# Retention and a top-1 mixture of experts on one core: logits with tokens on partitions, an ordered TensorE stream, joined routing, VectorE work spread over both products

## The chip, the cores and the metric

One core of a Trainium2 chip runs the whole program. The metric is the device time of one execution in microseconds (us). Engines are named as in the profile: PE is TensorE (PEld its loads of the stationary operand), DVE is VectorE, ACT is ScalarE, POOL is GpSimd, SP is SyncE, whose queue issues most DMAs.

## What is computed

The reference is a retention layer in blocks of 64, written here without its tables, followed by a mixture of eight experts of which each token takes one:

```python
# batch 4, heads 8, seq 768, head_dim 64; all float32
for b in range(nb):
    qb, kb, vb = (q[:, :, sl], k[:, :, sl], v[:, :, sl])
    intra = (qb @ kb.T * Dmask) @ vb
    inter = (qb * lam_pow) @ kv_state
    out[:, :, sl] = intra + inter
    kv_state = lam_block * kv_state + (kb * rev_pow).T @ vb
x = out.transpose(0, 2, 1, 3).reshape(3072, 512)
logits = x @ w_gate                       # 512 x 8
e_idx = argmax(logits); gate_w = softmax(logits)[e_idx]
eom = 1 / (1 + exp(-(x @ w_output_gate)))
for e in range(8):                        # w1: 512 x 1024, w2: 1024 x 512
    mask = e_idx == e
    out[mask] = gate_w * eom[mask, e] * (relu(x[mask] @ w1[e]) @ w2[e])
```

By the reference's own draw of the inputs the eight experts have 385, 361, 364, 401, 418, 380, 356 and 407 tokens.

## The kernel before

**Retention.** The sequence is cut into 6 chunks of 128 tokens; with 4 batches that makes 24 positions n = 4c + b. A loop over s from -2 to 21 (L1022 on) works on three positions at once, and its tail (L1091 on) does the last ones. An iteration transposes k and q of position s+2 on PE into `pk` and `pq` (`stage_a`, L308), and ACT copies them to `kT` (L315) and `qT` (L317). `stage_d` (L425) makes the gate's logits of position s-1: four products in four column groups of 32, summed later; ACT copies them (`part`, L434). `stage_a2` leaves `qd` (L328) and `kd` (L282) to POOL. `stage_b` (L346) makes the scores of s+1 in two banks, which DVE multiplies by the decay (`at`, L355, two instructions). `stage_e` turns the logits with one PE transpose (L456) and sums the four groups on DVE (L457). `stage_d2` turns x on DVE (L443) and stores it with four SP issues (L448). `stage_c` then adds state times `qd` (L379, not in the first chunk) and v times `at` (L384) in the bank `po`, ACT copies that to `xT` (L392), and PE makes the next state (`pst`, L401), which DVE joins with the old one (L412, L414).

Each engine takes its instructions in program order, so this order is the schedule; Python lists `later` and `ranking`, emptied by `weave`, drop the small routing instructions between the larger ones.

**Routing.** After every fourth position `route_choose` (L467) finds each token's expert on DVE as a one-hot `oh`, casts it and adds it up position by position in `cum` (L497, four adds); `route_place` (L519) gets each token's place in its expert's list from two PE products (`pr`: L535 with the triangle, L536 with ones and `cum`) and scatters a record to a table in HBM. After position 15 `pick_first` (L623, `pfirst`) takes the expert with most tokens so far; its weights are loaded first, and its first 256 columns gathered and turned ahead of the rest (`first_gather` L753, `first_turn`, `first_hi`, `first_lo`). The other seven are sorted by their counts at the end (`sort_rest`).

**Experts.** Every expert p has a fixed number of columns, `CAPS[p]` (L18). The sizes are for the order of picking. Products are made of two parts of each operand, a high one rounded by ACT (L129 for weights, L814 for x, L842 for h) and the rest from DVE (L138, L815, L843), in three products (`mm3`, L78 to L80). Up products fill `ph` in eight steps fc; down products of the experts 1 to 4 are in a turned form, four steps of 24 products of the expert's columns into `py` (read by DVE in L904 and L910), the others give rows of 128 tokens (`pyr`, 512 columns). The next expert's x is turned by `x_turn` (L796) and cut by `x_split` (L814, L815) in the steps of the down product. A token beyond an expert's columns goes to a block after everything (L1232 on) that runs only if a count is over its size.

**Handover** (L1091 to L1164). The first expert's products are a list of units; `fill` puts some of them between the last positions and routing steps.

Of the kernel before, what the change touches and what calls it, by code (L numbers as in the profile page):

```python
# [17 lines left out]
CAPS = (512, 434, 418, 402, 396, 384, 374, 368)  # L18
# [5 lines left out]
def kernel(  # L24
# [17 lines left out]
    P = 128  # L42
# [102 lines left out]

    qkv = {}
    packs = {}
    EARLY = 16


    BLOCKS = (0, 2, 3, 6, 9, 12, 15)

    def load_qkv(n, i0=0, i1=3):
# [4 lines left out]
        if n < EARLY and n not in packs:  # L158
            packs[n] = wpool.tile([P, 4, 512], F32, tag=("whi", "wlo")[n % 2], bufs=4, name=f"qkv_{n}")
        for i, (nm, src) in list(enumerate((("k", k), ("q", q), ("v", v))))[i0:i1]:  # L160
            t = packs[n][:, i, :] if n < EARLY else slot(f"{nm}_{n}")
            rows = src[b, :, c * P : (c + 1) * P, :]
            if nm == "q" and n in BLOCKS:
# [9 lines left out]
    with tc.manual_schedule():  # L173
# [19 lines left out]
        wgs = const.tile([P, NKC, 32], F32, name="wgs")  # L193
        nc.gpsimd.memset(wgs, 0.0)
# [16 lines left out]
    cum = const.tile([P, B + 1, E], BF16, name="cum")  # L211
# [28 lines left out]
    def routing_tables():  # L240
# [16 lines left out]
        nc.gpsimd.memset(cum[:, 0, :], 0.0)  # L257
# [27 lines left out]
    def query_parts(n, pq):  # L285
        if n not in BLOCKS:
            yield slice(0, P), lambda t: t, pq.rearrange("p (g t) -> p g t", g=NPAIR)
            return
# [8 lines left out]
    def stage_a(n):  # L297
# [4 lines left out]
        for src, dst in ((k_in, pk), (q_in, pq)):  # L302
            if n < 2 and (n > 0 or dst is pq):
                keep_warm(1)
            if dst is pq and n in BLOCKS:
                src = src.rearrange("p (h d) -> p h d", h=H)
# [9 lines left out]
        for r, view, src in query_parts(n, pq):  # L316
            nc.scalar.copy(out=view(qT[r]), in_=src)  # L317
        live[n] = dict(kT=kT, qT=qT, qd=None, kd=None)

    def stage_a2(n):  # L320
# [4 lines left out]
        if c > 0:  # L325
            qd = packs[n][:, 3, :] if n < EARLY else slot(f"qd_{n}")
# [43 lines left out]
    def stage_c(n):  # L370
        L = live[n]
        c, b = divmod(n, B)
        vt = qkv[n][2]
        sd = old_state.pop(n, None)
        po = bank(f"po_{n}")

        if c > 0:
            for g in range(NPAIR):
                nc.tensor.matmul(  # L379
                    po[:, g * P : (g + 1) * P], state[b][:, g, :], L["qd"][:, g, :], start=(g == 0), stop=False  # L380
                )
        for g in range(NPAIR):
# [9 lines left out]
        nc.scalar.copy(  # L392
            out=xT.rearrange("p (b g r) -> p g b r", b=4, g=NPAIR),
            in_=po.rearrange("p (g b r) -> p g b r", g=NPAIR, b=4),
        )
# [22 lines left out]
    parts = {}  # L418

    def stage_d(n):  # L420
        xT = live[n]["xT"]
        xTv = xT.rearrange("p (b g r) -> p g b r", b=4, g=NPAIR)
        plg = bank(f"plg_{n}")
        for g in range(NPAIR):
            nc.tensor.matmul(  # L425
                plg[32 * g : 32 * (g + 1), 0:P],
                wgs[:, g, :],
                xTv[:, g],
                start=True,
                stop=True,  # L430
                tile_position=(0, 32 * g),
            )
# [445 lines left out]
    def out_index(p):  # L878
# [6 lines left out]
        if rest:  # L885
            nc.gpsimd.memset(oi, 4 * NOROW)
# [436 lines left out]
```

## Time and profile before

| | before |
|---|---|
| median of 3 runs | 454.27 us (454.0, 454.27, 456.28) |
| the profiled execution | 455.79 us |
| its span | 453.9 us |
| PE busy | 422.8 us, 93% |
| DVE, ACT, POOL busy | 301.5, 191.6 and 263.0 us |
| retention and routing, start of the last position's state product | 143 us |
| first expert's first up product on the second half of its columns | 172.1 us |
| start of the last DMA-only stretch (end of PE) | 448.0 us |

Times in rows of the profile are us from the span's start. A group row reads: line, engine, operation, output <- input, sizes, count | busy us, mean ns of one | idle time of its engine just before and what ended it. A row of the chain reads start, length, engine, tile and line; the count behind it is of passes, and a float32 product has two.

### The profile page before, as it was taken

What the parts mean: (1) busy time and instruction counts of PE and PEld (TensorE: products, weight loads), DVE (VectorE), ACT (ScalarE), POOL (GpSimd) and SP (SyncE); (2) the same over time, 40 slices, a digit from 0 to 9 for tenths busy, and PEclk for the clock granted to TensorE, in tenths of its full rate; (3) what the DMA queues carried; (4) which work ended last, traced back from release to release, by engine and by line L of the source; (5) the groups of instructions that cost most, each with busy time, mean ns of one, the idle gap of its engine ahead of it and who ended that gap; (6) DMA issues with size and microseconds to landing.
All of it is one profiled execution on the core that took longest, in us unless ns stands there. A gap on an engine that the chain in (4) does not pass through costs nothing.

```text
span 453.9 us, 9333 instructions
## 1 busy us (share of the span) xinstructions
PE 422.8 (93%) x3282; PEld 383.2 (84%) x3282; DVE 301.5 (66%) x826; ACT 191.6 (42%) x461; POOL 263.0 (58%) x297
## 2 busy tenths in 40 slices
PE   8798999999939999999999989998998999999994
PEld 5687878887838879899999978997997988988984
DVE  4567586878587954765975686579559676684611
ACT  4554665665705512524344153434424453461400
POOL 6263656674564657774577477757757777412002
PEclk9998999999969999999999998999999999999999
DMA  7998787896993344574464344435534556533001
GB/s 172 223 235 217 192 207 196 199 216 168 200 259 128 92 116 175 152 256 144 124 231 146 116 137 143 140 124 179 196 123 141 173 198 226 175 124 123 16 26 47
DMA packets 109834, 73.21 MB, mean 161 GB/s; under 512 B 76708, under 2 KB 90792, under 8 KB 109777
## 3 DMA queue, kind: packets, MB, share of 16 engines
q1 hardware_dynamic: 101648, 56.07, 44.6%
q0 software_dynamic: 7984, 16.44, 11.3%
q8 instruction: 28, 0.46, 0.4%
q14 instruction: 30, 0.24, 0.2%
q10 hardware_dynamic: 144, 0.00, 0.0%
HBM read 59.47 MB, written 13.62 MB: 161 GB/s over the span
## 4 chain that ended last, share of the span: by engine, by line
PE 61%; DVE 19%; DMA 6%; issue 5%; ACT 4%; POOL 4%; SPq 0%; DVEq 0%; POOLq 0%; ACTq 0%
PE ph_None L79 8%; PE ph_None L80 8%; PE ph_None L78 8%; PE pyr L79 4%; PE pyr L80 4%; PE pyr L78 4%; PE po L384 4%; DVE wlo L138 3%; DVE cum L497 3%; PE po L379 3%; PE ps L346 3%; POOL out_dram L921 2%; DMA out_dram<-yo,outrow 2%; PE pk L308 2%; PE pst L401 2%
## 5 line engine op out<-in xcount | busy, mean ns | idle before, releaser
L732 POOL DMA_INDIRECT xg<-x_d,rows x90 | 94.8, 1053 | 45.5 <-issue 22.6
L79 PE MATMUL ph_None<-xlo,whi 128*128 128x434 f32 (+6 forms) x224 | 77.9, 348 | 5.4 <-DVE xlo L815 5.4
L138 DVE TENSOR_TENSOR wlo<-raw,whi 128x512 fp32r<-128x512 f32 x121 | 80.8, 688 | 1.4 <-ACT whi L129 0.8
L78 PE MATMUL ph_None<-xhi,whi 128*128 128x434 f32 (+6 forms) x224 | 77.8, 347 | 1.2 <-ACT xhi L814 1.2
L80 PE MATMUL ph_None<-xhi,wlo 128*128 128x434 f32 (+6 forms) x224 | 77.3, 345 | 0.0
L129 ACT CAST whi<-raw 128x512 fp32r<-128x512 f32 x128 | 75.1, 614 | 0.0
L921 POOL DMA_INDIRECT out_dram<-yo,outrow x54 | 57.9, 1073 | 16.4 <-issue 14.0
L842 ACT ACTIVATE hhi<-ph_None 128x434 fp32r<-128x434 f32 (+6 forms) x56 | 28.1, 502 | 91.0 <-PE ph_None L80 91.0
L843 DVE SCALAR_TENSOR_TENSOR hlo<-ph_None,hhi 128x434 fp32r<-128x434 f32 (+6 forms) x56 | 32.0, 571 | 51.6 <-ACT hhi L842 51.6
L79 PEld LDWEIGHTS ph_None<-xlo,whi 128*128 128x128 f32 x224 | 42.8, 191 | 7.2 <-DVE xlo L815 6.6
L78 PEld LDWEIGHTS ph_None<-xhi,whi 128*128 128x128 f32 x224 | 42.7, 191 | 3.3 <-ACT xhi L814 2.5
L79 PE MATMUL py<-hlo,whi 128*128 128x434 f32 (+3 forms) x128 | 45.0, 351 | 0.0
L80 PE MATMUL py<-hhi,wlo 128*128 128x434 f32 (+3 forms) x128 | 44.9, 351 | 0.0
L78 PE MATMUL py<-hhi,whi 128*128 128x434 f32 (+3 forms) x128 | 44.9, 351 | 0.0
L80 PEld LDWEIGHTS ph_None<-xhi,wlo 128*128 128x128 f32 x224 | 42.7, 191 | 0.3
L814 ACT CAST xhi<-y 128x256 fp32r<-128x256 f32 (+3 forms) x56 | 17.4, 360 | 58.2 <-DVE y L802 54.8
L985 POOL DMA_INDIRECT out_dram<-yn,table x12 | 13.2, 1098 | 48.5 <-DVE yn L982 37.7
L79 PE MATMUL pyr<-wlo,hhi 128*128 128x512 f32 (+1 forms) x96 | 37.6, 392 | 0.0
L78 PE MATMUL pyr<-whi,hhi 128*128 128x512 f32 (+1 forms) x96 | 37.6, 391 | 0.0
L80 PE MATMUL pyr<-whi,hlo 128*128 128x512 f32 (+1 forms) x96 | 37.5, 390 | 0.0
L584 POOL DMA_INDIRECT tab_d<-rec,idx x24 | 24.5, 1019 | 21.0 <-issue 19.2
L355 DVE TENSOR_TENSOR at<-ps,decay 128x512 f32<-128x512 f32 x48 | 31.7, 684 | 6.3 <-PE ps L346 6.1
(173 smaller groups left out, 849.9 us busy)
## 6 DMA issues: line engine op xcount, KB each, us to landing
raw<-in_moe_w_dram SPq DMA_DIRECT2D x27, 1024.0 KB, 5.2
x_d<-xn SPq DMA_DIRECT2D x80, 64.0 KB, 2.6
qkv<-in_k_dram SPq DMA_DIRECT2D x16, 256.0 KB, 3.1
qkv<-in_v_dram SPq DMA_DIRECT2D x16, 256.0 KB, 4.4
raw<-in_moe_w_dram POOLq DMA_DIRECT2D x3, 1024.0 KB
qkv<-in_q_dram SPq DMA_DIRECT2D x9, 256.0 KB, 4.0
k<-in_k_dram SPq DMA_DIRECT2D x8, 256.0 KB, 3.5
q<-in_q_dram SPq DMA_DIRECT2D x8, 256.0 KB, 3.8
```

The source lines that it names most:

```text
L78: nc.tensor.matmul(ps, a[0], b[0], start=first, stop=False)
L79: nc.tensor.matmul(ps, a[0], b[1], start=False, stop=False)
L80: nc.tensor.matmul(ps, a[1], b[0], start=False, stop=last)
L129: nc.scalar.copy(out=hi, in_=src)
L138: eng.tensor_tensor(out=lo, in0=src, in1=hi.bitcast(F32), op=ALU.subtract)
L355: nc.vector.tensor_tensor(out=at, in0=ps.rearrange("p (g t) -> p g t", g=NPAIR), in1=dec[:, j], op=ALU.mult)
L384: nc.tensor.matmul(po[j * D : (j + 1) * D, g * P : (g + 1) * P], vt[:, 2 * g + j, :], L["at"][j][:, g, :], start=(c == 0), stop=(c == 0 or ...
L584: nc.gpsimd.indirect_dma_start(out=tab_d, out_offset=bass.IndirectOffsetOnAxis(ap=idx, axis=0), in_=rec, in_offset=None, bounds_check=P * ...
L732: nc.gpsimd.indirect_dma_start(out=xg[(p, b // 4)][:, (b % 4) * P : (b % 4 + 1) * P], out_offset=None, in_=x_q, in_offset=bass.IndirectOff ...
L842: nc.scalar.activation(out=hi[:, r], in_=ph[:, r], func=AF.Relu)
L843: nc.vector.scalar_tensor_tensor(out=lo[:, r], in0=ph[:, r], scalar=0.0, in1=hi[:, r].bitcast(F32), op0=ALU.max, op1=ALU.subtract,)
L921: nc.gpsimd.indirect_dma_start(out=out.rearrange("t (q f) -> (t q) f", q=4), out_offset=bass.IndirectOffsetOnAxis(ap=ogs[p][0][:, b : b + ...
```

## The change

1. **Sizes.** `CAPS` becomes 448, 432, 416, 400, 400, 384, 368, 368.
2. **Logits.** The stationary operand is now `xT` (128 tokens), the moving one the 16 gate columns; the four products add up in the first 16 columns of `po`, after `xT` has been copied from it. `plg`, `part`, the transpose and the DVE sum go; DVE copies 128x16. `xT` is written as it lies in `po`, and `stage_d2` turns it through rearranged views.
3. **PE's order.** `stage_c` is split: `stage_c1` (state times `qd`) stands between the logits and the scores.
4. **q.** Every position's q is loaded in two block DMAs and copied by ACT in four 64x256 copies (before, seven positions were). Loads run ahead by one more position from s = 6 and two more from s = 11.
5. **Routing.** `oh` is written as bf16; `cum` is one row of sums. `pr` takes the counts of the earlier positions of the four from products of ones with their one-hots, and one reduce and one add bring `cum` up to date. `route_choose` is done at once in its iteration and `pr` at the end of the same iteration; `pick_first`, the first expert's register load and the weight loads come up to an iteration earlier.
6. **Splits.** L138 for pieces 0, 1 and 3 of the first expert's weights moves from POOL to DVE; in the handover several steps change places.
7. **Experts.** `out_index`, `count_over` and the first half of the next expert's `x_turn` and `x_split` move into the up product (fc 1 to 7), the rest into the down product's steps but the last; `down_banks` at fc 3.

```diff
-CAPS = (512, 434, 418, 402, 396, 384, 374, 368)
+CAPS = (448, 432, 416, 400, 400, 384, 368, 368)
...
-            if nm == "q" and n in BLOCKS:
+            if nm == "q":
...
+    def stage_c1(n):
...
+        po = L["po"] = bank(f"po_{n}")
+        if c > 0:
+            for g in range(NPAIR):
+                nc.tensor.matmul(
+                    po[:, g * P : (g + 1) * P], state[b][:, g, :], L["qd"][:, g, :], start=(g == 0), stop=False
+                )
...
-        nc.scalar.copy(
-            out=xT.rearrange("p (b g r) -> p g b r", b=4, g=NPAIR),
-            in_=po.rearrange("p (g b r) -> p g b r", g=NPAIR, b=4),
-        )
+        nc.scalar.copy(out=xT, in_=po)
...
-        plg = bank(f"plg_{n}")
+        lgt = live[n]["po"][:, 0 : 2 * E]
+        xTv = live[n]["xT"].rearrange("p (g t) -> p g t", g=NPAIR)
         for g in range(NPAIR):
-            nc.tensor.matmul(
-                plg[32 * g : 32 * (g + 1), 0:P],
-                wgs[:, g, :],
-                xTv[:, g],
-                start=True,
-                stop=True,
-                tile_position=(0, 32 * g),
-            )
-        part = small.tile([P, P], F32, tag="part", name=f"part_{n}")
-        nc.scalar.copy(out=part, in_=plg[:, 0:P])
+            nc.tensor.matmul(lgt, xTv[:, g], wgs[:, g, :], start=(g == 0), stop=(g == NPAIR - 1))
...
-        nc.tensor.transpose(out=pl, in_=part, identity=ident)
-        nc.vector.tensor_reduce(
+        nc.vector.tensor_copy(out=lgs[c][:, b, :], in_=live[n].pop("po")[:, 0 : 2 * E])
...
-        def count(b):
-            vec.tensor_tensor(out=cum[:, b0 + b + 1, :], in0=cum[:, b0 + b, :], in1=oh[:, b, :], op=ALU.add)
...
+            for b in range(nb - 1):
+                n = nb - 1 - b
+                nc.tensor.matmul(
+                    pr[:, (b + 1) * E : nb * E].rearrange("p (b e) -> p b e", b=n),
+                    ones,
+                    oh[:, b, :].unsqueeze(1).broadcast_to([P, n, E]),
+                    start=False, stop=False,
+                )
...
-            if s >= 0 and s != RES + 2:
-                load_qkv(s + AHEAD, 0, 2)
-                load_qkv(s + AHEAD - 2, 2, 3)
+            if s >= 0:
+                load_up_to(s + AHEAD + (s >= 6) + (s >= 11))
...
-                for j in range(4):
-                    split_lo(0, j, nc.gpsimd)
...
+            if n >= 0 and n % B == B - 1:
+                at_once(route_choose(n + 1 - B, n + 1))
+                ranking = route_place(n + 1 - B, n + 1)
...
+            if RES + 4 <= s < RES + 6:
+                for j in range(2):
+                    split_lo(0, 2 * (s - RES - 4) + j)
...
+                    if fc == 1 and p in TURNED:
+                        out_index(p)
+                    if fc >= 4:
+                        for f in work[: (fc - 2) // 2]:
+                            f()
+                        work = work[(fc - 2) // 2 :]
...
-                for f in work[i * len(work) // ns : (i + 1) * len(work) // ns]:
+                m = max(ns - 1, 1)
+                for f in work[i * len(work) // m : (i + 1) * len(work) // m]:
                     f()
```

**PE, the middle of the loop (s = 10).** Before, PE's instructions from the end of position 9's state to the products of position 10 (`pk`, `pq` of position 12, logits of 9, scores of 11):

```order
L401 MATMUL pst_1115<-qkv_537,kd_868 64x64 x8
L308 MATMUL pk_1138<-ident,qkv_833 128x128 x4
L308 MATMUL pq_1139<-ident,qkv_833 128x128 x4
L425 MATMUL plg_1155<-xT_1113,wgs 32x128 x4
L346 MATMUL ps_0_1173<-qT_1046,kT_1045 128x128
L346 MATMUL ps_1_1174<-qT_1046,kT_1045 128x128
```

and, after three more such pairs of scores, the end of this stretch:

```order
L346 MATMUL ps_0_1173<-qT_1046,kT_1045 128x128
L346 MATMUL ps_1_1174<-qT_1046,kT_1045 128x128
L456 MATMUL plg_1155<-ident,part_1160 128x128
L379 MATMUL po_1195<-qkv_647,state_133 128x128 x4
L384 MATMUL po_1195<-at_0_1084,qkv_647 64x128
```

The same place of the changed kernel:

```order
L404 MATMUL pst_1117<-qkv_538,kd_875 64x64 x8
L309 MATMUL pk_1140<-ident,qkv_752 128x128 x4
L309 MATMUL pq_1141<-ident,qkv_752 128x128 x4
L427 MATMUL po_1062<-wgs,xT_1115 128x16 x4
L378 MATMUL po_1161<-qkv_649,state_134 128x128 x4
L347 MATMUL ps_0_1175<-qT_1052,kT_1051 128x128
L347 MATMUL ps_1_1176<-qT_1052,kT_1051 128x128
```

The transpose behind the scores is gone, and the state's product has moved ahead of them; v times `at` follows the scores directly.

**DVE, the routing of positions 16 to 19 (s = 20).** Before, the choice of the expert runs between the two halves of the scores' multiplication, and the counts follow the turn of x:

```order
L355 TENSOR_TENSOR at_0_2199<-ps_0_2172,decay 128x512
L507 TENSOR_REDUCE mx_2184<-lg_1876 128x4
L508 TENSOR_TENSOR d_2186<-lg_1876,mx_2184 128x32
L509 SCALAR_TENSOR_TENSOR cand_2187<-d_2186,erev 128x32
L355 TENSOR_TENSOR at_1_2204<-ps_1_2173,decay 128x512
L512 TENSOR_REDUCE cm_2185<-cand_2187 128x4
L513 TENSOR_TENSOR oh_2188<-cand_2187,cm_2185 128x32
L492 CAST ohb_2189<-oh_2188 128x32
L494 COPY cum<-cum 128x8
L443 STREAM_TRANSPOSE xn_2210<-xT_2109 128x512
L497 TENSOR_TENSOR cum<-cum,oh_2188 128x8 x4
```

The same place of the changed kernel:

```order
L356 TENSOR_TENSOR at_0_2151<-ps_0_2140,decay 128x512
L356 TENSOR_TENSOR at_1_2153<-ps_1_2141,decay 128x512
L489 TENSOR_REDUCE mx_2155<-lg_1875 128x4
L490 TENSOR_TENSOR d_2157<-lg_1875,mx_2155 128x32
L491 SCALAR_TENSOR_TENSOR cand_2158<-d_2157,erev 128x32
L494 TENSOR_REDUCE cm_2156<-cand_2158 128x4
L495 TENSOR_TENSOR oh_2159<-cand_2158,cm_2156 128x32
L438 STREAM_TRANSPOSE xn_2179<-xT_2094 128x512
L748 SCALAR_TENSOR_TENSOR first_rows_2185<-table_0_2030 128x2
L138 TENSOR_TENSOR wlo_2134<-raw_1917,whi_2133 128x512 x2
```

The choice now stands behind both halves, the adds to `cum` are gone from here, and two of the four subtractions that POOL had follow (the other two are in the next iteration).

**DVE, the end of the second expert's down product (p = 2).** Before, the last pieces of the third expert's x are in the fourth step, ahead of its weights' splits and the reading of `py`:

```order
L815 TENSOR_TENSOR xlo_1_3995<-y_1_4042,xhi_1_3994 128x160
L815 TENSOR_TENSOR xlo_2_3999<-y_1_4042,xhi_2_3998 128x160
L815 TENSOR_TENSOR xlo_3_4003<-y_1_4042,xhi_3_4002 128x160
L138 TENSOR_TENSOR wlo_4048<-raw_3840,whi_4047 128x512 x2
L904 STREAM_TRANSPOSE zt_3_4095<-py_3_3800 128x448
L910 TENSOR_TENSOR yo_0_3962<-zt_3_4095,outscale_3845 128x4x32
L910 TENSOR_TENSOR yo_1_3964<-zt_3_4095,outscale_3845 128x4x32
L910 TENSOR_TENSOR yo_2_3966<-zt_3_4095,outscale_3845 128x4x32
L910 TENSOR_TENSOR yo_3_3968<-zt_3_4095,outscale_3845 128x2x32
L843 SCALAR_TENSOR_TENSOR hlo_0_4157<-ph_0_None,hhi_0_4156 128x402
```

The changed kernel, from the last pieces of x (in the third step) to that step's reading of `py`:

```order
L816 TENSOR_TENSOR xlo_2_3835<-y_1_3916,xhi_2_3834 128x160
L816 TENSOR_TENSOR xlo_3_3839<-y_1_3916,xhi_3_3838 128x160
L138 TENSOR_TENSOR wlo_4004<-raw_3832,whi_4003 128x512 x2
L905 STREAM_TRANSPOSE zt_2_4009<-py_2_3741 128x416
L911 TENSOR_TENSOR yo_0_3927<-zt_2_4009,outscale_3676 128x4x32
```

and, behind three more such L911, its fourth step:

```order
L138 TENSOR_TENSOR wlo_4004<-raw_3832,whi_4003 128x512 x2
L905 STREAM_TRANSPOSE zt_3_4045<-py_3_3742 128x416
L911 TENSOR_TENSOR yo_0_3927<-zt_3_4045,outscale_3676 128x4x32
L911 TENSOR_TENSOR yo_1_3929<-zt_3_4045,outscale_3676 128x4x32
L911 TENSOR_TENSOR yo_2_3931<-zt_3_4045,outscale_3676 128x4x32
L911 TENSOR_TENSOR yo_3_3933<-zt_3_4045,outscale_3676 128x32
L844 SCALAR_TENSOR_TENSOR hlo_0_4104<-ph_0_None,hhi_0_4103 128x400
```

No instruction on the next expert's x is left behind the third step.

More of the change, by code (lines that the diff above doesn't have):

```diff
@@ L374, in stage_c @@
         sd = old_state.pop(n, None)
[L375 to L380, printed above, removed]
-                )
+        po = L["po"]
         for g in range(NPAIR):
@@ L626, in rank_keys @@
         )
-        return pc
     def expert_regs(p, in_i, n):
```

198 lines of the change are left out of this document (98 added, 100 removed).

## The prediction, before the result

> **What bounds the kernel now.** I began with busy times and the chain that ended last: PE is busy for 93% of the span, and its work and the waits on DVE make up most of that chain.
>
> ```profile
> PE 422.8 (93%) x3282; PEld 383.2 (84%) x3282; DVE 301.5 (66%) x826; ACT 191.6 (42%) x461; POOL 263.0 (58%) x297
> PE 61%; DVE 19%; DMA 6%; issue 5%; ACT 4%; POOL 4%; SPq 0%; DVEq 0%; POOLq 0%; ACTq 0%
> ```
>
> So the time is PE's work plus its waits, and 31 us (453.9 less 422.8) is what all PE waits can be worth, the end included. A steady position of the retention loop, from the chain of waits cut to 5.11 us, is PE from end to end:
>
> ```profile
> 88.67 0.89 PE po L379 x8
> 89.56 1.02 PE po L384 x16
> 90.58 0.47 PE pst L401 x16
> 91.05 0.59 PE pk L308 x4
> 91.64 0.44 PE pq L308 x4
> 92.07 0.36 PE plg L425 x8
> 92.43 1.09 PE ps L346 x16
> 93.52 0.26 PE plg L456
> ```
>
> There, only a change in PE's own passes counts. The waits of PE, summed by what they wait for (total, times, longest), show where it stands still:
>
> ```profile
> PE pr L536 <- DVE cum L497: 9.5, 3, 7.1
> PE ph_None L79 <- DVE xlo L815: 5.4, 3, 1.8
> PE plg L456 <- ACT part L434: 2.5, 5, 0.5
> ...
> PE pfirst L623 <- DVE cum L497: 0.7, 1, 0.7
> ```
>
> **The stall at 125 us** is the largest. The timeline shows DVE's choice of the expert, then four small adds (L497) beside a POOL that runs without a pause:
>
> ```profile
> 122.02 0.17 DVE L507 TENSOR_REDUCE mx<-lg 128x4 f32<-128x32 f32 x1
> ...
> 123.38 0.19 DVE L513 TENSOR_TENSOR oh<-cand,cm 128x32 f32<-128x32 f32 x1
> ...
> 124.39 8.07 DVE L497 TENSOR_TENSOR cum<-cum,oh 128x8 bf16<-128x8 bf16 x4
> ...
> 124.48 1.28 POOL L328 TENSOR_TENSOR qd<-qT,qdec 128x512 f32<-128x512 f32 x1
> ...
> 125.70 4.91 POOL L138 TENSOR_TENSOR wlo<-raw,whi 128x512 fp32r<-128x512 f32 x4
> ...
> 132.31 0.19 PE L536 MATMUL pr<-cum,ones 128*128 128x32 bf16 x1 [7.08 <-DVE cum L497]
> ```
>
> Adds of 8 columns take 2 us each there: they stand behind POOL's instructions. By the Trainium skill, "SBUF — State Buffer", section "SBUF: two separate sides", a VectorE instruction with two SBUF inputs and a GpSimd instruction that reads SBUF exclude each other for the whole instruction; the trace agrees here with 8.07 us for four adds. Behind such stalls the granted clock (the column after the five busy columns) is lower:
>
> ```profile
> 35.00:45.00 10.00, 8.12 (x96) 7.12 (x93) 7.24 (x25) 4.44 (x15) 3.40 (x5) 0.83 0.87 212
> 130.00:140.00 10.00, 7.69 (x64) 6.81 (x64) 6.11 (x20) 1.66 (x6) 2.51 (x6) 0.61 1.04 304
> ```
>
> The first stands around another wait for L497, the second behind this one.
>
> **The change, part by part.**
>
> *Logits.* Each position loses .36 (L425) and .26 (L456), in sum .62 us. It gains four float32 products, eight passes, with a stationary operand of 128 columns and only 16 moving ones. The nearest row is L379: the same stationary operand, .89 for eight passes, .111 each. Whether 16 columns instead of 128 shorten a pass isn't in the trace. I take .89, since a pass that changes a 128-column operand has nothing shorter here: +.27 a position, times 24 = **+6.5**. The lower end is the old product's own .36 (8 passes over 32-column operands): -.26 x 24 = -6.2, that is 12.7 us less than I take. By the Trainium skill, "TensorE: Matmul & The Clock Gate", section "LDWEIGHTS (loading the stationary operand)", a load takes its columns divided by 1.2 in ns, whatever the rows; eight loads of 128 columns would be an estimated .85 us, and the sum 1 us lower. That rule speaks against this part of the change, and no row of this case has so short a product behind a float32 load.
>
> The transpose's wait for ACT goes with it: **-2.5**. `qd` is needed one score product (1.09) earlier, and is made an iteration ahead.
>
> *Routing.* The waits for L497 end: 9.5 + .7 = **-10.2**. The dips of the clock behind them end too: (1 - .83) x 8.12 + (1 - .61) x 7.69 = **-4.4**. What is late next is `pr` itself, now in the same iteration as the choice. DVE does both halves of `at`, then the choice; PE meanwhile has v times `at` and the state:
>
> ```profile
> 94.07 1.29 DVE L355 TENSOR_TENSOR at<-ps,decay 128x512 f32<-128x512 f32 x2
> ...
> 122.57 0.68 DVE L355 TENSOR_TENSOR at<-ps,decay 128x512 f32<-128x512 f32 x1
> ```
>
> The choice takes 1.55 from L507 to the end of L513 (123.57), of which .6 was the half of `at` between them: .95. DVE needs 1.29 + .95 = 2.24 from the scores, PE has 1.02 + .47 = 1.49, so it waits .75. Behind it stand pk, pq, the logits and the scores of the next position. Three more small products of `pr` add at most .57 by L536's .19 each, less if they overlap; I take .25, and 1.0 for wait and products: 5 routings in the loop, **+5.0**. The ends are 0 (PE late enough) and 1.28 more for each (one POOL L328 that holds DVE, below).
>
> *Start.* q of the early positions takes one more SP issue, and PE waits once for such a load:
>
> ```profile
> 10.05 0.59 SPq L166
> 10.69 4.58 DMA qkv<-in_q_dram
> ```
>
> One more issue ahead: **+.6** (0 to 1.2). Later the loads run further ahead than before, so I give more SP work there no price.
>
> *ACT.* Four copies instead of one, at 17 positions:
>
> ```profile
> L317 ACT COPY qT<-pq 64x256 f32<-64x256 f32 x28 | 10.7, 384 | 2.1 <-PE pq L308 1.8
> L317 ACT COPY qT<-pq 128x512 f32<-128x512 f32 x17 | 10.0, 591 | 0.0
> L392 ACT COPY xT<-po 128x512 f32<-128x512 f32 x24 | 14.1, 586 | 49.2 <-PE po L384 48.0 <-issue 1.2
> ```
>
> 4 x .384 - .591 = +.95 us, beside an ACT that is busy for 4.44 of 10 us in the window above, or 2.3 of a position: cover enough, so nothing. Without cover it would be 17 x .95 = 16 us. DVE's moved subtractions and transposes are hidden likewise behind products in which DVE has idle time.
>
> *Handover.* With logits only after `xT`, the last position's logits have nothing to hide the copy, .59 by L392 and a start of .1; one routing wait in a place without cover I put at 1.0: **+1.7** (0 to 4).
>
> *Sizes.* Windows of products of one size each, 96 of them:
>
> ```profile
> 172.13:183.65 11.52, 11.52 (x98) 11.51 (x97) 6.07 (x13) 4.57 (x12) 8.83 (x9) 1.00 0.34 116
> 213.75:232.95 19.20, 19.20 (x98) 18.42 (x96) 16.87 (x56) 7.65 (x18) 10.89 (x11) 1.00 0.43 141
> 251.19:269.59 18.40, 18.40 (x97) 17.74 (x95) 14.05 (x55) 4.48 (x11) 10.42 (x12) 1.00 0.33 97
> 269.59:292.03 22.44, 19.99 (x97) 19.18 (x97) 14.79 (x36) 10.14 (x22) 17.57 (x17) 0.92 0.54 183
> 292.03:309.68 17.65, 17.65 (x98) 17.64 (x97) 12.30 (x44) 4.96 (x12) 11.52 (x12) 1.00 0.37 109
> 309.68:329.73 20.05, 17.93 (x97) 17.17 (x97) 14.55 (x36) 9.60 (x21) 15.52 (x15) 1.00 0.57 193
> 329.73:347.01 17.28, 17.28 (x98) 17.14 (x97) 11.96 (x43) 4.80 (x12) 11.42 (x12) 1.00 0.35 109
> 347.01:366.49 19.48, 17.42 (x97) 16.70 (x97) 14.30 (x32) 9.59 (x21) 15.10 (x15) 1.00 0.60 202
> 366.49:382.86 16.37, 16.37 (x74) 13.53 (x74) 12.67 (x28) 7.39 (x18) 12.83 (x12) 1.00 0.55 171
> ```
>
> In order: the first expert's second half (256 columns, .1200 us a product), p = 1 down (434, .2000), p = 2 down (418, .1917), p = 3 up (402) and down (.1839), p = 4 up (396) and down (.1800), p = 5 up (384) and down (72 products of 512, .2274). A line through 256 and 512 has .419 ns a column, and gives .1938 at 432, .1871 at 416, .1804 at 400. Up and down together are 192 products: p = 1 -1.19, p = 2 -.88, p = 3 -.67, p = 4 +.08. The first expert's second half falls from 256 to 192 columns; by the line .0932, but I stop at L379's .111, a pass with a 128-column operand: -.85 (by the line -2.6). In all **-3.5**.
>
> *Starts of the experts.* The up products of p = 3, 4, 5 begin with a wait for the last piece of their own x:
>
> ```profile
> 273.11 0.79 DVE L815 TENSOR_TENSOR xlo<-y,xhi 128x160 fp32r<-128x160 f32 x3
> ...
> 273.48 0.46 PE L79 MATMUL ph_None<-xlo,whi 128*128 128x402 f32 x1 [1.83 <-DVE xlo L815]
> ```
>
> That the wait costs more than the 5.4 us of the waits' list is seen from the windows: up less down of one size is 22.44 - 17.65 = 4.79 and 20.05 - 17.28 = 2.77, and for p = 5 19.48 - 96 x .1737 (the line at 384) = 2.80. The first has the clock at .92. The change finishes x one step earlier, some 4.5 us (a quarter of 17.65) against waits under 2, and half of it already in the up product: all three go, **-10.4**.
>
> *Sum*: 6.5 - 2.5 - 10.2 - 4.4 + 5.0 + .6 + 1.7 - 3.5 - 10.4 = -17.2. The profiled execution took 455.79 (span 453.9, 1.89 around it), 1.52 above the median of 454.27; so 438.6 against it, **437.1** on the median.
>
> **Rivals.**
>
> A. The logits are as cheap as the old product: 12.7 less, **424.4**. For it: fewer moving columns, and .36 for eight passes exists. Against it: those passes had 32-column operands.
>
> B. DVE is still held by POOL. The choice and the subtractions moved to DVE read two operands from SBUF, as the adds at 125 us did, and POOL still makes `qd` in each position. One L328 of 1.28 in each of five routings and 1.7 more in the handover is 8.1: **445.2**. Against it: POOL has lost the eight splits there, and the order puts less behind each other.
>
> C. The expert starts stay as late, because x's gathers or ACT's copies, not DVE's last steps, end last: +10.4, **447.5**. The list of waits names DVE, hence little chance.
>
> D, the other side: with 192 columns the products of the first expert's second half leave the fast rate. All products of the experts here have at least 256 columns; L379, a plain float32 product of 128 columns, takes two passes, .2225 for 128 columns. If 192 columns go at that rate, each costs .334 instead of .111, times 96 is +21.4: **458.5**. It decides from a size somewhere below 256, which no row shows. Against it: the time goes straight from 512 to 256 with no bend.
>
> **How the numbers follow.** Chances: forecast .56, A .17, B .12, C .06, D .07; .02 for anything else on the slow side, such as the block for tokens over a size (by the counts of the draw no size is exceeded: 407 in 448 for the first, then 418, 401, 385, 380, 364, 361, 356 in 432 down to 368). The range of 425 to 449 takes in the forecast, B and C, with the part of A whose price lies between its ends, about .82. A measurement can tell 0.5%, 2.3 us. The forecast, A, B and C are all faster than that (.91); B and C with a further loss come within 2.3 us of 454.27, for which I move .05 to no change; D and the rest are slower: faster .86, same .05, slower .09.
>
> **What would show it.** Right: no wait of PE for DVE at `pr` over 2 us, a granted clock near 1 behind 125 us, a steady position of about 5.4 us with .9 in L427, first products of p = 3 to 5 without a wait, windows of .187 us a product at 416 columns. Wrong: L427 well under .5 (A), DVE instructions of 32 columns that take over 1 us beside POOL (B), waits for `xlo` or `xhi` at the experts' starts (C), 96 products of 192 columns in over 20 us instead of 10.7 (D).

## The result, and the profile after

The changed kernel took 439.30 us (437.93 to 440.99, 4 runs) beside 454.44 us for the kernel before (454.0 to 456.28, 4 runs): a ratio of 0.9661, 95% interval 0.9618 to 0.9704. The profiled execution took 439.35 us, with a span of 437.7 us, 16.2 less than before.

PE's busy time is the same as before, 422.5 against 422.8 us, so nearly all of the 16.2 us went from the time in which PE stands still, 31.1 us before and 15.2 now. That the busy sums are equal is chance: as the rows below show, the products of the retention became longer and those of the experts shorter. From the page, and from the waits of PE (total, times, longest):

```profile
PE 422.5 (97%) x3281; PEld 395.0 (90%) x3281; DVE 286.0 (65%) x806; ACT 204.0 (47%) x488; POOL 253.1 (58%) x283
...
PE pr L516 <- DVE oh L495: 5.3, 5, 1.3
...
PE pfirst L623 <- DVE oh L495: 0.8, 1, 0.8
PE po L427 <- ACT xT L398: 0.7, 1, 0.7
```

Of the five waits at `pr`, four stand in the loop (.87 to 1.34 us) and one in the handover (1.17 us at 138.06); the loop's fifth routing waits at `pfirst` instead. The forecast had five in the loop, of .75. There is no wait for `xlo`, and none for `part` or a q load. A steady position, in the chain of waits:

```profile
85.08 0.59 PE pk L309 x4
85.66 0.44 PE pq L309 x4
86.10 0.80 PE po L427 x8
86.90 0.99 PE po L378 x8
87.88 1.09 PE ps L347 x16
88.97 1.02 PE po L390 x16
90.00 0.46 PE pst L404 x16
```

It starts the next position after 5.38 us (before: 5.11). The choice of the expert for positions 16 to 19, the five instructions of DVE ahead of `pr`, runs without a stop:

```profile
123.72 0.18 DVE L489 TENSOR_REDUCE mx<-lg 128x4 f32<-128x32 f32 x1
123.92 0.19 DVE L490 TENSOR_TENSOR d<-lg,mx 128x32 f32<-128x32 f32 x1
124.15 0.19 DVE L491 SCALAR_TENSOR_TENSOR cand<-d,erev 128x32 f32<-128x32 f32 x1
124.38 0.19 DVE L494 TENSOR_REDUCE cm<-cand 128x4 f32<-128x32 f32 x1
124.60 0.19 DVE L495 TENSOR_TENSOR oh<-cand,cm 128x32 bf16<-128x32 f32 x1
```

The windows of the experts, in order: the first expert's second half (192 columns), p = 1 up (432), p = 2 down (416), p = 3 up and p = 4 up (400):

```profile
168.87:179.57 10.70, 10.70 (x98) 10.70 (x96) 5.50 (x12) 3.96 (x12) 8.18 (x9) 1.00 0.17 50
190.56:209.36 18.80, 18.80 (x97) 18.09 (x96) 12.49 (x38) 7.88 (x16) 10.48 (x11) 1.00 0.47 161
...
246.08:264.00 17.92, 17.92 (x97) 17.89 (x97) 14.31 (x40) 6.81 (x16) 14.21 (x13) 1.00 0.52 161
264.00:281.29 17.29, 17.29 (x98) 17.29 (x97) 12.89 (x41) 7.70 (x16) 13.11 (x13) 1.00 0.49 171
...
298.57:315.85 17.28, 17.28 (x98) 17.28 (x97) 12.87 (x41) 7.70 (x16) 13.36 (x13) 1.00 0.49 168
```

Up products now take as long as down products of the same size (18.80 for p = 1 and 17.28 for p = 3, down): no stall at an expert's start is left. One thing is worse than forecast. In the handover the granted clock is .5 for two windows:

```profile
136.70:140.11 3.41, 2.24 (x29) 1.86 (x27) 3.08 (x17) 1.88 (x6) 2.49 (x3) 1.00 0.90 306
140.11:143.53 3.42, 3.42 (x17) 3.42 (x17) 3.32 (x14) 0.00 (x0) 2.55 (x3) 0.50 0.03 3
143.53:146.94 3.41, 3.41 (x22) 3.32 (x22) 2.04 (x15) 1.74 (x5) 1.49 (x3) 0.50 0.61 162
```

By stretches, the two executions and the forecast compare so (pk(n) is the start of the k transposes of position n; the forecast's terms are put into the stretch where they belong):

| stretch | before, us | after, us | difference | forecast |
|---|---|---|---|---|
| start to pk(6) | 27.88 | 27.80 | -0.1 | +0.9 |
| pk(6) to pk(23) | 94.54 | 97.19 | +2.7 | +3.1 |
| pk(23) to the first product of p = 1 | 72.13 | 65.58 | -6.6 | -8.2 |
| from there to the end of the span | 259.35 | 247.13 | -12.2 | -13.0 |
| sum | 453.9 | 437.7 | -16.2 | -17.2 |

Of the logits, three positions fall into the first stretch, 17 into the second and four into the third; of the 2.5 us of waits for `part`, .5 into the first and 2.0 into the second. The first stretch is good to 1.3 us only: it takes 27.31 us in memset_dve and 26.55 in dve_split (below), whose kernels are there the same as the one before.

### The profile page after: what moved, and what is told of

Its sections match the earlier page's. It is cut to its first block, busy times and chain, and to the rows that moved or that the text cites. A ratio compares the mean times of both kernels' runs of the same rounds, so it can differ in the third digit from the quotient of the medians.

```text
span 437.7 us, 9355 instructions
## 1 busy us (share of the span) xinstructions
PE 422.5 (97%) x3281; PEld 395.0 (90%) x3281; DVE 286.0 (65%) x806; ACT 204.0 (47%) x488; POOL 253.1 (58%) x283
## 4 chain that ended last, share of the span: by engine, by line
PE 92%; DVE 4%; DMA 1%; issue 1%; ACT 1%; SPq 0%; POOL 0%; POOLq 0%; DVEq 0%
PE ph_None L80 9%; PE ph_None L78 9%; PE ph_None L79 9%; PE py L80 5%; PE py L78 5%; PE py L79 5%; PE ps L347 5%; PE pyr L78 5%; PE pyr L79 5%; PE pyr L80 5%; PE po L427 4%; PE po L390 4%; PE po L378 4%; PE pk L309 3%; PE pq L309 2%; PE ph L78 2%
## 5 line engine op out<-in xcount | busy, mean ns | idle before, releaser
L138 DVE TENSOR_TENSOR wlo<-raw,whi 128x512 fp32r<-128x512 f32 x128 | 84.8, 685 | 0.6 <-ACT whi L129 0.5
L80 PE MATMUL ph_None<-xhi,wlo 128*128 128x400 f32 (+4 forms) x224 | 76.2, 340 | 0.0
L78 PE MATMUL ph_None<-xhi,whi 128*128 128x400 f32 (+4 forms) x224 | 76.2, 340 | 0.0
L79 PE MATMUL ph_None<-xlo,whi 128*128 128x400 f32 (+4 forms) x224 | 76.2, 340 | 0.0
L922 POOL DMA_INDIRECT out_dram<-yo,outrow x53 | 57.4, 1084 | 16.1 <-issue 12.2
L844 DVE SCALAR_TENSOR_TENSOR hlo<-ph_None,hhi 128x400 fp32r<-128x400 f32 (+4 forms) x56 | 31.8, 569 | 36.8 <-ACT hhi L843 36.4
L80 PE MATMUL py<-hhi,wlo 128*128 128x400 f32 (+2 forms) x128 | 44.5, 347 | 0.0
L78 PE MATMUL py<-hhi,whi 128*128 128x400 f32 (+2 forms) x128 | 44.5, 347 | 0.0
L79 PE MATMUL py<-hlo,whi 128*128 128x400 f32 (+2 forms) x128 | 44.5, 347 | 0.0
L318 ACT COPY qT<-pq 64x256 f32<-64x256 f32 x96 | 36.9, 385 | 1.6 <-PE pq L309 0.7
L78 PE MATMUL pyr<-whi,hhi 128*128 128x512 f32 (+2 forms) x96 | 37.6, 392 | 0.0
L79 PE MATMUL pyr<-wlo,hhi 128*128 128x512 f32 (+2 forms) x96 | 37.5, 391 | 0.0
```

Of the source, the lines that this page charges most:

```text
L78: nc.tensor.matmul(ps, a[0], b[0], start=first, stop=False)
L79: nc.tensor.matmul(ps, a[0], b[1], start=False, stop=False)
L80: nc.tensor.matmul(ps, a[1], b[0], start=False, stop=last)
L138: eng.tensor_tensor(out=lo, in0=src, in1=hi.bitcast(F32), op=ALU.subtract)
L844: nc.vector.scalar_tensor_tensor(out=lo[:, r], in0=ph[:, r], scalar=0.0, in1=hi[:, r].bitcast(F32), op0=ALU.max, op1=ALU.subtract,)
L922: nc.gpsimd.indirect_dma_start(out=out.rearrange("t (q f) -> (t q) f", q=4), out_offset=bass.IndirectOffsetOnAxis(ap=ogs[p][0][:, b : b + ...
```

## The experiments

Each ratio is to executions of the kernel before that ran beside it. It is worked out from the single times, so it need not be the quotient of the two medians. The changed kernel's own is 0.9661 (0.9618 to 0.9704).

| run | median, us | kernel before, us | ratio (95%) |
|---|---|---|---|
| logits_alone | 455.09 | 455.19 | 1.0007 (0.9969 to 1.0045) |
| old_logits | 441.79 | 455.19 | 0.9704 (0.9656 to 0.9752) |
| pr_later | 440.63 | 455.19 | 0.9698 (0.9673 to 0.9723) |
| x_late | 438.86 | 455.19 | 0.9662 (0.9636 to 0.9688) |
| memset_dve | 447.18 | 454.92 | 0.9843 (0.9784 to 0.9903) |
| dve_split | 450.72 | 454.92 | 0.9881 (0.9808 to 0.9954) |
| pool_split | 443.64 | 454.92 | 0.9741 (0.9681 to 0.9801) |
| hand_order | 443.40 | 454.92 | 0.9721 (0.9648 to 0.9794) |
| pr_table_again | 435.54 | 454.72 | 0.9605 (0.9561 to 0.9648) |

Three more (memset_pool, pr_table, hand_table) stand beside a kernel before that itself took 506.93 us (496.73 to 516.23); they come last.

### x_late: is it the place of the next x?

```diff
-                    if fc >= 4:
-                        for f in work[: (fc - 2) // 2]:
-                            f()
-                        work = work[(fc - 2) // 2 :]
...
-                m = max(ns - 1, 1)
-                for f in work[i * len(work) // m : (i + 1) * len(work) // m]:
+                for f in work[i * len(work) // ns : (i + 1) * len(work) // ns]:
```

> The changed kernel with the next expert's x turned and cut as before, all in the down product's steps, up to the last. If that place made the waits at the experts' starts, three waits for xlo of about 2 us come back, and with what stands around them 10.4 us: about 450. If sizes or the moved out_index did it, 440 or less.

It took 438.86 us, the same as the changed kernel, and none of the three stalls came back. Its up products of p = 3, 4 (400 columns) and 5 (384):

```profile
261.98:279.26 17.28, 17.28 (x97) 17.28 (x97) 11.54 (x38) 7.08 (x14) 13.37 (x13) 1.00 0.49 169
...
296.54:313.82 17.28, 17.28 (x97) 17.28 (x97) 12.04 (x39) 7.08 (x14) 13.36 (x13) 1.00 0.52 172
...
331.10:347.74 16.64, 16.64 (x97) 16.64 (x97) 10.05 (x20) 7.00 (x14) 12.98 (x13) 1.00 0.53 177
```

The last three pieces of `xlo` for p = 3 stand in DVE's order where they stood before, but DVE is on time: they start at 259.87, 2.1 us ahead of the first product of p = 3. Before, they started at 273.11, 3.5 us behind the start of that product's window (269.59). So the forecast's reason for its largest term of the experts is wrong. What delays DVE in the kernel before is seen further up its queue. In DVE's waits (total, times, longest) stands:

```profile
DVE outrow L893 <- POOL outrow L886: 9.2, 3, 3.4
```

and in its timeline, at the start of the down product of p = 2:

```profile
255.69 0.22 DVE L893 TENSOR_SCALAR outrow<-token 32x13 int32<-32x13 f32 x2 [2.40 <-POOL outrow L886]
```

`out_index` lets POOL fill `outrow` (L886) before DVE writes it; POOL has scatters of about 1 us each ahead of that fill, and DVE stands for it, 2.4 us here and 9.2 us in three places. DVE then runs after PE through the whole down product, and reaches the last `xlo` late.

### memset_dve: that fill alone

```diff
-            nc.gpsimd.memset(oi, 4 * NOROW)
+            nc.vector.memset(oi[:, full:nb], 4 * NOROW)
```

> The kernel before with one edit: outrow is filled by DVE (its last column only), not by POOL. In the kernel before, DVE stands idle 2.40 us for POOL at that fill at the start of the down product of p = 2 and is late from there on. If that made the waits for xlo at the starts of p = 3 to 5, they go without any move of x, by up to 10.4 us: 444. If x has to be finished a step earlier for that, or its place in the up product frees DVE, the waits stay: 454.

One line of the change, in the kernel before, took it to 447.18 us, a ratio of 0.9843 (0.9784 to 0.9903). The stretch from the first product of p = 1 to the end is 250.72 us, 8.6 less than before and 3.6 more than after. Its up products of p = 3 and p = 4 (402 and 396 columns) are nearly as short as the down ones; they had been 22.44 and 20.05 us:

```profile
268.25:287.08 18.83, 17.92 (x98) 17.57 (x97) 13.21 (x34) 8.06 (x16) 14.79 (x14) 1.00 0.50 171
...
304.72:322.30 17.58, 17.58 (x97) 17.58 (x96) 11.68 (x28) 7.07 (x14) 13.93 (x13) 1.00 0.51 169
```

1.2 us are left at p = 3, where `out_index` and `count_over` still stand at the start of p = 2's down product; with 2.3 us for the sizes (below) that is 3.5 of the 3.6. So POOL's fill made all of the stalls but these 1.2 us, which x_late, with `out_index` and `count_over` moved, doesn't have either; which of the two made them is not shown. Moving x added nothing that a run can show.

### pool_split and dve_split: does POOL hold DVE?

The first puts the four subtractions of piece 0 back on POOL in the changed kernel, the second takes them to DVE in the kernel before:

```diff
+            if s == RES + 4:
+                for j in range(4):
+                    split_lo(0, j, nc.gpsimd)
...
-            if RES + 4 <= s < RES + 6:
-                for j in range(2):
-                    split_lo(0, 2 * (s - RES - 4) + j)
```
```diff
-            if s == RES + 4:
-                for j in range(4):
-                    split_lo(0, j, nc.gpsimd)
...
+            if RES + 4 <= s < RES + 6:
+                for j in range(2):
+                    split_lo(0, 2 * (s - RES - 4) + j)
```

> The changed kernel with the four subtractions for piece 0 on POOL again, in the iteration s = 20, where the choice of positions 16 to 19 now runs on DVE. If POOL holds DVE's instructions with two SBUF inputs, d, cand and oh wait for POOL up to 1.28 us each and pr by 2 to 4 us more, with the clock halved behind it: 442 to 446. If the gain came from taking cum's adds out of pr's way, nothing changes: 439.

> The kernel before with one edit: the four subtractions for piece 0 (L138) run on DVE, two each in the iterations s = 20 and 21, and not on POOL. If the adds to cum took 8.07 us because POOL held the port, they take under 2 us, the wait of 7.1 us for pr falls to at most 3 (two splits of .69 may stand ahead of it) and the half clock behind it goes (3.0): 446. If the adds are slow by themselves, or if something else is as late there, it stays at 453 to 455.

pool_split took 443.64 us, 4.3 more than the changed kernel by the medians, within what was expected if POOL holds DVE; the intervals of the ratios overlap, but the rows show the mechanism. The same five instructions as above, now beside POOL:

```profile
122.54 4.96 POOL L138 TENSOR_TENSOR wlo<-raw,whi 128x512 fp32r<-128x512 f32 x4
123.69 0.18 DVE L489 TENSOR_REDUCE mx<-lg 128x4 f32<-128x32 f32 x1
123.91 1.19 DVE L490 TENSOR_TENSOR d<-lg,mx 128x32 f32<-128x32 f32 x1
...
125.13 1.19 DVE L491 SCALAR_TENSOR_TENSOR cand<-d,erev 128x32 f32<-128x32 f32 x1
126.35 0.19 DVE L494 TENSOR_REDUCE cm<-cand 128x4 f32<-128x32 f32 x1
126.58 0.97 DVE L495 TENSOR_TENSOR oh<-cand,cm 128x32 bf16<-128x32 f32 x1
...
127.60 0.21 PE L516 MATMUL pr<-oh,tri 128*128 128x32 bf16 x1 [4.12 <-DVE oh L495]
```

The two reductions, with one input from SBUF, keep their .18 and .19; the three instructions with two inputs from SBUF go from .19 to 1.19, 1.19 and .97, about one POOL instruction each. By the Trainium skill, "SBUF — State Buffer", section "SBUF: two separate sides", a VectorE instruction with two SBUF inputs and a GpSimd instruction that reads SBUF exclude each other; the trace agrees, .18 with one such input beside 1.19 with two. PE's wait is 4.12, and the clock is halved for 10.24 us from 126.94 on.

dve_split took 450.72 us, a ratio of 0.9881 (0.9808 to 0.9954); the 446 expected lies just below that interval. The wait of 7.1 us became 3.3 (at most 3 expected), and the half clock behind it shrank from 10.24 to 3.41 us but did not go, while PE waited 1.2 us more for a load of k. The adds are still slow where POOL still works, at `qd`:

```profile
125.81 3.01 DVE L497 TENSOR_TENSOR cum<-cum,oh 128x8 bf16<-128x8 bf16 x3
...
130.04 0.16 DVE L497 TENSOR_TENSOR cum<-cum,oh 128x8 bf16<-128x8 bf16 x1
```

1 us each beside POOL, .16 alone. Both parts of the change are needed here: the splits away from POOL, and the adds away from `pr`.

### logits_alone and old_logits: the price of the new logits

logits_alone is the kernel before with the edits of part 2 of the change. old_logits is the changed kernel with these undone; in its handover two of the first expert's products move between the logits' transposes:

```diff
-        fill(2)
+        fill(1)
         stage_d(n)
+        fill(1)
         stage_e(n - 1)
+        fill(1)
         stage_e(n)
-        fill(4)
+        fill(3)
```

> The kernel before with part 2 alone: logits with xT as the stationary operand, in the first columns of po, no part, no transpose. If a pass costs its 128-column operand (.89 us for eight, as forecast), the steady position grows from 5.11 to about 5.38 us, 24 x .27 = +6.5, less the 2.5 us of waits for part: about 4 us slower than before, 458. If passes with 16 moving columns are cheap (.36), about 8 us faster, 446.

> The changed kernel with the logits of before (four column groups, part, transpose, DVE sum) in its own order, in which the state's product stands between logits and scores. If the new logits are a price that the rest pays for, it is faster than the changed kernel by 24 x .27 = 6.5 us, about 433, and no wait for part appears, since 2 us of products cover ACT's copy. If the new logits pay for themselves (by ACT's and DVE's saved work in the handover), it is at 439 or above.

Both expectations from the pass prices failed: logits_alone took 455.09 us, no change (458 expected), and old_logits 441.79, not faster than the changed kernel (433 expected). From the chain of waits of logits_alone, a position from the logits on:

```profile
88.97 0.80 PE po L418 x8
89.77 1.09 PE ps L345 x16
90.86 1.09 PE po L378 x8
```

and from that of old_logits:

```profile
86.49 0.36 PE plg L429 x8
86.85 1.09 PE po L379 x8
87.93 1.09 PE ps L348 x16
89.03 0.26 PE plg L463
```

The same eight passes of state times `qd` take .89 behind the transpose (before), .99 behind the new logits (after), and 1.09 behind the scores or behind the four narrow column groups. So in these rows a product's price depends on what stands ahead of it: logits, transpose, state and scores together take 2.60 before, 2.88 after, 2.98 in logits_alone and 2.80 in old_logits. In the changed kernel's order the new logits cost .08 a position more than the old ones, 2 us in all, not the 6.5 of the forecast; the rest of the .28 is the order's. In old_logits these 2 us do not come out. From pk(6) to pk(23) it takes 97.37 us, beside 97.19 in the changed kernel; among its waits are 1.6 us for `part` (none in the changed kernel) and 1.5 at `pfirst` (.8). From there to p = 1 it takes 67.81, beside 65.58, with a wait of 1.6 us for `ez` and half clock twice for 3.41 us. Its wait of 2.4 us at `pcount` is not the logits' alone: x_late, with the new logits, has one of 1.9.

logits_alone's positions are .37 longer than before (5.48), some 8 us in all, and yet it lost nothing. Its trace has no waits for `part`, one for `cum` of 6.6 us and one for `ohb` of 1.9 instead of three of 9.5 in sum, and stalls at the starts of p = 4 and 5 of 1.0 and 1.3 us from product to product instead of 2.3 and 2.2. Which of these come from the edit and which are the chance of one execution I did not separate.

### pr_later, hand_order and pr_table_again: what binds the handover

pr_later calls the block that makes `pr` one iteration later, behind `stage_d`:

```diff
+            if ranking:
+                first_steps = pick_first() if s == RES + 1 else []
+                for f in first_steps[:1] + ranking[:1]:
+                    f()
+                later.extend(mixed(first_steps[1:], ranking[1:]))
+                ranking = []
             if s >= 0:
                 stage_c1(s)
...
-            if ranking:
-                first_steps = pick_first() if s == RES else []
...
-                ranking = []
             if s == RES + 2:
```

> The changed kernel with pr not at the end of the iteration of its choice but in the next one, behind pk, pq and the logits. If the five waits of about 1.1 us at pr are waits for DVE's choice alone, they vanish behind 2 us of products: 5.3 us less, about 434. If the later record makes the first expert's weights, scatters or gathers late, the time goes back in the handover: 438 or above.

All five waits at `pr` went, and pk(23) came 4.3 us earlier, at 120.67. But the time was 440.63 us: the first product of p = 1 starts at 190.66, as in the changed kernel (190.57). The gain was given back within the handover, at the gather of the first expert's x. The rows of SP, DVE and POOL in pr_later:

```profile
123.27 0.36 SPq L702 DMA_DIRECT2D table<-tab_d  x1
...
128.39 0.16 DVE L748 SCALAR_TENSOR_TENSOR first_rows<-table 128x2 int32<-128x2 int32 x1 [5.74 <-DMA table<-tab_d]
129.37 1.50 POOL L754 DMA_INDIRECT xg<-x_d,first_rows  x1 [9.15 <-PE po L390]
```

A first reading was PE's order. hand_order is pr_later with these edits:

```diff
-        stage_d(n - 2)
         stage_c1(n - 1)
+        stage_d(n - 2)
...
         stage_e(n)
-        fill(4)
+        fill(8)
...
             split_lo(1, j)
-        fill(6)
+        fill(2)
```

> The changed kernel with pr later (as pr_later) and two more changes of PE's order in the handover: the state's product of position 22 ahead of the logits that wait for xT, and four more products of the first expert ahead of pcount (fill 8 and 2 for 4 and 6). If pr_later gave its 4 us back only because PE's order put waiting instructions ahead of ready ones in the handover, the waits of 1.0 and 1.9 us there go: 437 to 438, below the changed kernel. If the handover is bound by DVE's chain of routing steps, the waits move behind these products and it stays at 439 to 441.

It took 443.40 us, above both expectations. The wait at `pcount` went, but PE waited 1.8 us for `xg` and 1.4 for `wlo`, and the clock was halved for 13.65 us from 135.92 on. So PE's order alone was not it. The rows above name another reason: the gather waits for a small table whose load stands in SP's queue behind the first expert's second weight piece. (The gather's row names PE as what ended its wait, but in the changed kernel, in pr_later and in the next run it starts .98 us after `first_rows`, which it reads.) pr_table_again is pr_later with these two exchanged:

```diff
             if s == RES + 2:
+                load_outs(0, 0, 2)
                 load_piece(1)
-                load_outs(0, 0, 2)
```

> pr_table once more, on another chip: pr later, and the routing table's load ahead of the second weight piece in SP's queue. If the gather of the first expert's x binds the handover, its first instruction on POOL starts 2 to 5 us before 129, PE's wait of 1.4 us for xg goes, and of the 4.3 us that pr_later gained by position 20 at least 2 stay: 437 to 438, below the changed kernel. If DVE's routing steps of the last positions bind it, PE waits for them instead and the time stays at 440.

The same rows of SP, DVE and POOL:

```profile
120.69 0.37 SPq L702 DMA_DIRECT2D table<-tab_d  x1
...
122.53 0.16 DVE L748 SCALAR_TENSOR_TENSOR first_rows<-table 128x2 int32<-128x2 int32 x1
...
123.51 1.53 POOL L754 DMA_INDIRECT xg<-x_d,first_rows  x1 [3.53 <-PE pr L526]
```

It took 435.54 us, 0.9605 (0.9561 to 0.9648): clear of pr_later, below the 437 to 438 expected, and 3.8 us below the changed kernel by the medians, though the intervals overlap. The table is issued 2.6 us earlier and used 1.8 us after its issue, not 5.1 us behind a megabyte of weights; the gather starts 5.9 us earlier. Its profiled execution has no half clock before the end of PE; that of pr_later has two stretches of 3.41 us, and how much of the gain is theirs is not separated. A wait of 2.1 us at `pcount` remains.

### Three runs without a verdict

memset_pool is the changed kernel with POOL's fill back, pr_table the same kernel as pr_table_again, hand_table is hand_order with SP's exchange.

> The changed kernel with POOL filling outrow again (the whole tile), at its new place in step fc = 1 of the up product. If DVE's wait for that fill was harmful because it stood at the start of the down product, where DVE has no slack, the wait of about 2.4 us shows in DVE's row but PE does not stop: 439. If DVE can't afford it in the up product either, PE waits for hlo or xlo at p = 1, 3 and 4 by 1 to 2.5 us each: 442 to 447.

> pr_later with two lines of SP's queue exchanged: the load of the routing table (L702) ahead of the first expert's second weight piece (L114), which stands there until its buffer is free. If pr_later gave its 4 us back because the first expert's gather lands at the same time whatever PE does (its POOL instruction starts at 129.0 in the changed kernel and 129.4 in pr_later, after the table), the gather starts 2 to 5 us earlier, the wait of 1.4 us for xg goes and the time falls to 437 to 438. If DVE's routing steps bind the handover, only the wait moves: 440.

> hand_order with the same exchange in SP's queue. If the half clock of 13.65 us in hand_order came from the 2.6 us that PE stood waiting for the gather, it shrinks to at most 7 us and the time falls by 4 to 6 us to 437 to 439 or less. If the order of the handover itself starves DVE or ACT, it stays at 442 to 443.

They took 514.82, 506.72 and 504.64 us; the intervals of their ratios are 1.0014 to 1.0525, 0.9960 to 1.0144 and 0.9895 to 1.0154. With the kernel before at 506.93 us, PE in these traces stands for "issue" by up to 1.8 us a time in the experts, and nothing of 1% can be read from their times; for the second kernel, pr_table_again has the times beside a kernel before of 454.72.

What memset_pool was for can be read from its trace all the same. In the up product of p = 3, POOL's fill stands behind a row of scatters, DVE waits for it, and PE for DVE:

```profile
322.62 0.97 POOL L922 DMA_INDIRECT out_dram<-yo,outrow  x1 [0.30 <-issue]
323.58 0.14 POOL L887 MEMSET outrow<- 128x13 int32 x1
...
323.75 0.22 DVE L894 TENSOR_SCALAR outrow<-token 32x12 int32<-32x12 f32 x2 [15.15 <-issue]
...
325.65 0.70 PE L78 MATMUL ph_None<-xhi,whi 128*128 128x400 f32 x1 [7.16 <-DVE outscale L898]
```

The same comes again at p = 4, with 13.87 us for DVE and 6.62 for PE; the traces of pr_table and hand_table, beside the same kernel before, have no such waits. So the fill on POOL is not harmless in the up product either. What it would cost at the usual times is not measured.

## Why the prediction was right, and where it was not

The forecast was 437.1 us and the kernel took 439.30. Over the stretches the sum of -17.2 met -16.2; the rest of the miss is in the step to the median, for which 1.52 us were taken off, while the changed kernel's profiled execution lies only .05 above its median. That the sum came so close is partly luck: the first two stretches came out 1.0 and .4 us better than forecast, the other two 1.6 and .8 worse. By its steps:

- **Logits.** +.27 a position was forecast and +.27 came (5.11 to 5.38), but by luck. The eight passes took .80, not .89, and state times `qd`, whose move ahead of the scores the forecast put at nothing, rose from .89 to .99. By old_logits, .20 of the .28 is the price of the order and .08 that of the new logits. The reading that a pass that changes a 128-column operand "has nothing shorter here" overlooks the scores: 16 passes with operands of 64 rows and 128 columns in 1.09 us. The lower end, .36 for eight passes (rival A), is far off. By the Trainium skill, "TensorE: Matmul & The Clock Gate", section "LDWEIGHTS (loading the stationary operand)", the estimate worked out from the page's rule was .85; the measured .80 is a little below it.
- **Routing.** Right, step by step. The waits for L497 are gone, and a position with `pr` takes 6.48 instead of 5.39 us, five times: 5.5 against 5.0. DVE's choice took 1.07 us (123.72 to 124.79), not .95, and all products of `pr` .14 together, where .25 was put for the added ones. pool_split shows the cause, and that rival B is real where POOL has its splits; without them it didn't happen.
- **Start.** +.6 was forecast for one more issue. Instead the wait of 1.7 us for a q load is absent, and the stretch to pk(6) is the same as before, within the 1.3 us by which it differs from one execution to another.
- **Handover.** The stretch fell 1.6 us less than forecast. The +1.7 for two waits came about as worked out: .71 for the copy of `xT` (130.67) and 1.17 at `pr` (138.06). The mis-sized term is the -4.4 for the clock. The two dips it counted are gone, but a new one of 6.83 us appeared at 140.11, behind a window, with the wait at `pr` in it, in which PE was busy for 2.24 of 3.41 us. The profiled execution of x_late, the same kernel up to the second half of the first expert, has no such dip; it starts that half at 166.84, not 168.87, and takes 63.71 us from pk(23) to p = 1, 1.9 less than the changed kernel and 8.4 less than the one before. Yet the dip doesn't explain the miss of the median: the other three executions of the changed kernel have a mean clock of .997 to .999, beside .988, and took 437.93 to 440.99. Why they are no faster stays open.
- **Sizes.** -3.5 forecast. By the windows: first expert's second half 11.52 to 10.70, -.8; p = 1 .2000 to .1958, -.8; p = 2 .1900 (up) and .1917 (down) to .1867, -.8; p = 3 .1839 to .1800, -.7; p = 4 none. In all -3.1, of which 2.3 behind the first expert. From p = 6 on it takes some .5 us more than before (71.6 against 71.0), which no term of the forecast has and no run explains. Rival D is out: 192 columns take .1115 a product, the floor taken from L379 (.111), neither the line's .0932 nor .334.
- **Starts of the experts.** The step that failed in its reason: "The change finishes x one step earlier [...]: all three go". All three went, and 12.2 less 2.3 for the sizes is 9.9 against 10.4. But this is luck in the reason: x_late shows that finishing x earlier did not do it, and memset_dve that the fill of `outrow`, which the forecast did not price, did most of it (8.6). The forecast read what PE waited for, and not what had made that DVE instruction late; rival C had the same blind spot.

## What to carry to other kernels

When an engine waits for an instruction, follow that engine's own queue back to its last idle stretch: here DVE's wait of 2.4 us for a fill on POOL, a whole product earlier, was the cause of a stall of 4.8 us on PE, and one line took away all but 1.2 us of that. Two terms of one sum can be right in size for a wrong reason, so undo one edit at a time before keeping a reason. A gain in one stage lasts only if the next one can start earlier: look at the issue order of the small loads it depends on.

## What the runs showed of the hardware that I had not expected

- The same eight float32 passes (L379 and its like) take .89 us (before), .99 (after) or 1.09 (logits_alone, old_logits) by what PE did just before.
- Ahead of the end of PE, the halved clock lasts 3.41, 6.83, 10.24 or 13.65 us in these traces, multiples of 3.41, and it follows windows of that length in which PE was busy for 30% (124.21 to 127.63, before) to 66% (136.70 to 140.11, after); in another window of the changed kernel (123.04 to 126.46), with 61%, it did not follow.
- A load of a few bytes a row was used 1.8 us after its issue ahead of a megabyte (pr_table_again), and 5.1 us after it behind one (pr_later).
- A fill of .14 us on POOL behind a row of scatters of about 1 us each held DVE for 2.4 us (before) and for 15.15 us (memset_pool).
